# Leftover queries of two visits scored as one block in four 64x64 array tiles, ahead of the whole blocks

## The chip, the cores and the metric

One core of a Trainium2 chip. The metric is the device time of one execution in microseconds. Executions of this kernel agree within about 0.6%.

## The reference

Thresholded attention, then an MLP with a squared ReLU, all fp32:

```python
# q, k, v: (8, 8, 576, 64); tau = 0.02; w_in: (512, 2048); w_out: (2048, 512)
scores = q @ k.T / 8
scores = where(scores >= max(scores) - tau, scores, -1e9)
attn = exp(scores - max(scores)); attn = attn / (sum(attn) + 1e-9)
x = (attn @ v) -> (4608, 512)          # heads side by side
out = maximum(x @ w_in, 0) ** 2 @ w_out
```

576 queries are four whole blocks of 128 and 64 left over. That leftover is what the change is about.

## The kernel before

The work is cut into *visits*: two heads of one batch element each. A visit (from visit 8 on; the first eight are parts of visits) has five *steps*, one per block of queries: 0 to 3 are whole (128 queries of each of two heads, 64x128 array tiles), 4 is the leftover (64 queries of both heads at once, as one whole-array product with a block-diagonal `qmid`). MLP work of earlier tokens ("pieces") is spread between the steps; for all but the first *chunk* of 256 tokens, the output matrix product is made of seven smaller *products* on quarters of the matrices, of which two read `gsum`, sums that POOL makes of the squared hidden values, and two more a `gsum` that DVE makes anew. From visit 11 on the attention weights are not transposed by TensorE: DVE transposes 32x32 blocks into `turned`, and SP's queue places them in `wT` by many small transfers; four steps after a visit's last block its *mix* multiplies `wT` by v. `wT` exists once, so the next visit's placements wait for that mix to have read it.

```python
def scores(s):
    ...
    for half, u in halves:                       # two halves of 288 keys
        if i < NBLK:
            rows, lhsT = slice(u * D, (u + 1) * D), qT[u * D:(u + 1) * D, i * P:(i + 1) * P]
        else:
            rows, lhsT = slice(0, P), qmid       # leftover: whole array, half of it zeros
        nc.tensor.matmul(sc[u][:, half, 0:HALF], lhsT, kT[rows, half * HALF:(half + 1) * HALF], ...)
...
def place_blocks(vis, pair):                     # 16 transfers for blocks 0+1, 2+3, leftover each
    wb = blocks[vis, pair]
    for qb in range(4):
        for j in range(4):
            ...
            nc.sync.dma_start(out=to[:, :, at:at + 64], in_=wb[rows, j::4, :, :]...)
...
# in the loop over steps s; (m, x) is the step before
if s in mixes ...: mix(*mixes[s])                # the mix follows the scores of its step
...
turn_blocks(m, x)
if x >= 2:
    place_blocks(m, x - 2)                       # 0+1 after block 2, 2+3 after block 3, leftover last
```

## Time and profile before

| | before |
|---|---|
| time, median of 3 (later 4) | 1436.16 (1436.39) us |
| profiled span | 1426.6 us |
| TensorE (PE) busy | 1369.2 us, 96% |
| DVE, ACT, POOL busy | 62%, 31%, 63% |
| PE's wait for `wT` placed by SP, as the waits name it | 7.7 us in 5 waits |

PE is the engine to read. A line of the timeline is "start, duration, engine, source line, operation, tiles, array rows*columns, shape, count, [idle before, released by]". Durations of matmuls overlap in the pipeline and their ends are modelled, so work is priced by the distance from one start to the next.

### The profile page before, as it was taken

The page shows a single profiled execution, that of the slowest core. Times are in us where ns is not written, and L with a number is a line of the kernel's source. Part 1 is how long each engine was busy: PE and PEld are TensorE (multiplying, and loading weights), DVE is VectorE, ACT ScalarE, POOL GpSimd, SP SyncE. Part 2 cuts the span into 40 slices and gives each one's busy share as a digit, 9 for nine tenths or more (in the row PEclk, how much of TensorE's full clock was granted, in tenths as well). Part 3 has the DMA queues.
Part 4 walks back from the last instruction along what each step waited for, and adds up shares of the span by engine and source line. Part 5 has one row for each costly group of instructions (what it writes and reads, how often), then busy time and mean ns, then how long its engine had stood idle before and what let it go on. Part 6 is the DMA issues. An engine that isn't in the chain of part 4 may idle for free.

```text
span 1426.6 us, 22558 instructions
## 1 busy us (share of the span) xinstructions
PE 1369.2 (96%) x7460; PEld 1058.5 (74%) x7460; DVE 886.2 (62%) x1922; ACT 440.5 (31%) x1080; POOL 900.2 (63%) x1215
## 2 busy tenths in 40 slices
PE   5898989999999999999999999999999999999998
PEld 3676556777777777777777787777777877778887
DVE  5999986975767766757666666666666666401011
ACT  3766654222222323222232222322222232200100
POOL 2688888757676766766576757585667575422322
PEclk9999999999999999999999999999999999999999
DMA  7664431435455555554445454544444545310000
GB/s 150 131 141 115 126 101 46 83 72 98 92 104 95 110 98 107 97 110 86 93 85 106 94 108 94 107 87 98 82 101 91 109 97 104 67 30 8 8 15 16
DMA packets 397604, 127.16 MB, mean 89 GB/s; under 512 B 381488, under 2 KB 386288, under 8 KB 397488
## 3 DMA queue, kind: packets, MB, share of 16 engines
q1 hardware_dynamic: 377008, 93.02, 34.4%
q0 software_dynamic: 18096, 32.40, 8.3%
q8 instruction: 60, 0.98, 0.3%
q10 hardware_dynamic: 2384, 0.30, 0.1%
q14 instruction: 56, 0.46, 0.1%
HBM read 49.81 MB, written 9.44 MB: 42 GB/s over the span
## 4 chain that ended last, share of the span: by engine, by line
PE 78%; DVE 8%; SPq 5%; issue 3%; ACT 2%; POOL 2%; DMA 2%; POOLq 0%; DVEq 0%; ACTq 0%
PE bank L417 30%; PE bank L484 25%; PE s L212 11%; PE bank L374 10%; SPq L329 3%; SPq L337 2%; DVE st L217 2%; DVE w L240 2%; DVE turned L138 1%; DMA wT<-turned 1%; PE bank L276 1%; PE bank L451 1%; ACT w L228 1%; DVE turned L137 1%; POOL w L252 1%
## 5 line engine op out<-in xcount | busy, mean ns | idle before, releaser
L417 PE MATMUL bank<-xT,w_in_sb 128*128 128x256 f32 x2304 | 519.5, 382 | 1.6 <-ACT osb L458 1.6
L417 PEld LDWEIGHTS bank<-xT,w_in_sb 128*128 128x128 f32 x2304 | 431.9, 190 | 81.6 <-issue 21.1
L217 DVE TENSOR_REDUCE st<-s 128x1 f32<-128x576 f32 x288 | 206.6, 752 | 204.2 <-PE s L212 203.3
L240 DVE SCALAR_TENSOR_TENSOR w<-s,st,w 128x576 f32<-128x576 f32 x269 | 210.1, 814 | 121.6 <-ACT w L228 121.3
L484 PE MATMUL bank<-wo,gsum 128*128 128x256 f32 x1088 | 250.7, 384 | 4.5 <-POOL gsum L407 4.3
L252 POOL TENSOR_SCALAR w<-w,st 128x576 f32<-128x576 f32 x269 | 227.1, 851 | 26.2 <-DVE st L243 18.2
L484 PEld LDWEIGHTS bank<-wo,gsum 128*128 128x128 f32 x1088 | 205.5, 191 | 43.5 <-issue 7.1
L428 POOL TENSOR_TENSOR g<-g 128x512 f32<-128x512 f32 x144 | 152.2, 1061 | 108.3 <-ACT g L427 107.5
L225 ACT ACTIVATE st<-st 128x2 f32<-128x2 f32 (+1 forms) x160 | 32.7, 204 | 602.2 <-DVE st L217 601.6
L212 PE MATMUL s<-kT,qT 64*128 64x288 f32 x1024 | 175.7, 438 | 33.3 <-DVE w L240 16.8
L316 DVE STREAM_TRANSPOSE turned<-w 128x64 f32<-128x64 f32 (+2 forms) x400 | 173.8, 487 | 27.3 <-DMA wT<-turned 21.9
L484 PE MATMUL bank<-wo,g 128*128 128x256 f32 x816 | 187.9, 381 | 0.0
L228 ACT ACTIVATE w<-s,st 128x576 f32<-128x576 f32 x269 | 184.5, 731 | 0.6 <-issue 0.3
L374 PE MATMUL bank<-wT,vs 128*64 128x128 f32 (+7 forms) x1700 | 172.9, 356 | 10.8 <-DMA wT<-turned 7.7
L484 PEld LDWEIGHTS bank<-wo,g 128*128 128x128 f32 x816 | 153.5, 190 | 28.1 <-issue 6.4
L212 PEld LDWEIGHTS s<-kT,qT 64*128 64x128 f32 x1024 | 98.9, 190 | 93.7 <-issue 64.4
L374 PEld LDWEIGHTS bank<-wT,vs 128*64 128x64 f32 (+1 forms) x1700 | 100.6, 136 | 84.3 <-issue 37.1
L250 POOL TENSOR_SCALAR st<-st 128x2 f32<-128x2 f32 (+1 forms) x160 | 38.3, 239 | 168.6 <-DVE w L240 156.8
L427 ACT ACTIVATE g<-bank 128x512 f32<-128x512 f32 x144 | 86.1, 599 | 180.7 <-PE bank L417 180.2
L498 DVE TENSOR_TENSOR gsum<-g 128x512 f32<-128x512 f32 x34 | 22.6, 698 | 108.9 <-PE bank L484 108.9
L195 POOL COPY qmid<-qT 64x64 f32<-64x64 f32 x64 | 19.4, 303 | 84.2 <-DVE qT L191 82.3
L174 POOL DMA_DIRECT2D kl<-in_k_dram x100 | 69.6, 699 | 0.0
(70 smaller groups left out, 1109.5 us busy)
## 6 DMA issues: line engine op xcount, KB each, us to landing
wT<-turned SPq DMA_DIRECT2D x800, 72.0 KB, 2.2
out_dram<-osb POOLq DMA_DIRECT2D x34, 256.0 KB, 2.8
wo<-in_moe_w_in_dram SPq DMA_DIRECT2D x16, 512.0 KB, 4.6
wo<-in_moe_w_out_dram SPq DMA_DIRECT2D x16, 512.0 KB, 3.7
kl<-in_k_dram POOLq DMA_DIRECT2D x100, 72.0 KB, 2.6
ql<-in_q_dram POOLq DMA_DIRECT2D x100, 72.0 KB, 2.5
vs<-in_v_dram POOLq DMA_DIRECT2D x50, 128.0 KB, 3.5
wT<-turned SPq DMA_DIRECT2D x200, 20.0 KB, 1.9
```

Source lines behind the costliest of these rows:

```text
L174: nc.gpsimd.dma_start(out=to, in_=src)
L212: nc.tensor.matmul(sc[u][:, half, 0:HALF], lhsT, kT[rows, half * HALF:(half + 1) * HALF], start=True, stop=True)
L217: nc.vector.tensor_reduce(out=mx[:, u:u + 1], in_=sc[u][:, :, 0:HALF], axis=AX.XY, op=ALU.max)
L228: nc.scalar.activation(out=w[:, u, :].rearrange("p (h k) -> p h k", h=2), in_=sc[u][:, :, 0:HALF], func=AF.Exp, bias=bias[:, u:u + 1], sca ...
L240: nc.vector.scalar_tensor_tensor(out=wu, in0=sc[u][:, :, 0:HALF], scalar=thr[:, u:u + 1], in1=wu, op0=ALU.is_ge, op1=ALU.mult, accum_out=s ...
L252: nc.gpsimd.tensor_scalar(out=w[:, u, :], in0=w[:, u, :], scalar1=z[:, u:u + 1], scalar2=rcp[:, u:u + 1], op0=ALU.add, op1=ALU.mult)
L316: nc.vector.transpose(wb[:, at:at + k1 - k0, i % 2, :], w[:, u, k0 * 32:k1 * 32].rearrange("p (k q) -> p k q", q=32))
L374: nc.tensor.matmul(ps[u * D:(u + 1) * D, :], vs[n % 2][rows, u * (NBLK + 1) + c, :], wT[rows, NBLK if c == NBLK else u * (NBLK + 1) + c, a ...
L417: nc.tensor.matmul(h[:, x % 2, :], w_in_sb[:, c, f * P:(f + 1) * P], xT[:, c, at:at + TCH], start=(c == 0), stop=(c == NMC - 1))
L427: nc.scalar.activation(out=to, in_=h, func=AF.Relu)
L428: nc.gpsimd.tensor_tensor(out=to, in0=to, in1=to, op=ALU.mult)
L484: nc.tensor.matmul(to, left[:, f, :], wo[:, slot, f, :], start=(f == 0), stop=(f == HF - 1))
```

## The change

The visits 12 to 35 are taken in pairs. The leftovers of a pair (four heads, 64 queries each) become one step of two PSUM tiles, in four 64x64 array tiles: head u takes the rows, visit v the columns. It comes first of the pair's nine steps (ten before). For that q's leftover rows get loads of their own (`q_left`, 8 small ones a pair), k's transpose exists twice, `wT` gets 64 more columns so that the odd visit's leftover has its own place, loads and placements get an explicit schedule, and the ring of MLP inputs shrinks from six chunks to five to pay for the memory. Its core:

```diff
-    wT = const.tile([P, NC9, S], FP32, name="wT")
+    ODD, ONE, LEFT, TWO = 0, REST, REST + 2 * P, 2 * REST + 2 * P
+    wT = const.tile([P, NC9, S + REST], FP32, name="wT")
-    kT = const.tile([P, S], FP32, name="kT")
-    RING = 6 * TCH
+    kT = [const.tile([P, S], FP32, name=f"kT{i}") for i in range(2)]
+    RING = 5 * TCH
...
+        if i == NBLK and paired(vis):
+            for half in range(2):
+                for v_ in range(2):
+                    for u in range(2):
+                        rows, cols = slice(u * D, (u + 1) * D), slice(v_ * D, (v_ + 1) * D)
+                        term(u, half, rows, qmid[rows, cols], kT[v_], cols)
...
+    def paired(n):
+        return n >= 3 * HP
+    for n in range(len(visits)):
+        if paired(n):
+            visits[n] = visits[n][0], ([] if n % 2 else [NBLK]) + list(range(NBLK))
...
+            place_at[s + (2 if paired(n - 1) else 3)].append((n, 2, (0, 1)))
+            place_at[s + 3] += [(n, 2, (2, 3)), (n, 0)]
+            place_at[s + 5].append((n, 1))
+            place_at[s + 8].append((n + 1, 0))
+            place_at[s + 9].append((n + 1, 1))
...            (further: the schedule of loads and transposes, the layout in mix)
```

More of the change, by code (lines that the diff above doesn't have):

```diff
@@ L84 @@
     assert at + 2 * S <= 3 * HF * HD
+    q_left = const.tile([P, 2, REST // 32, 32], FP32, name="q_left")
     qT = const.tile([P, S], FP32, name="qT")
-    kT = const.tile([P, S], FP32, name="kT")
-    RING = 6 * TCH
+    kT = [const.tile([P, S], FP32, name=f"kT{i}") for i in range(2)]
+    RING = 5 * TCH
     xT = const.tile([P, NMC, RING], FP32, name="xT")
@@ L151, with rows_32 @@
     loads = deque()
+    def rows_32(t, n, m):
+        b, h = divmod(visits[n][0], HP)
+        return t[b, 2 * h + m // 2, :, (m % 2) * 32:(m % 2) * 32 + 32].rearrange("(c p) d -> p c d", p=32)
     def load_qk(n):
-        b, h = divmod(visits[n][0], HP)
-        h *= 2
+        if by_dma(n):
+            load_part(k, n)
+            load_part(q, n)
+            return
         for x, t in ((rows_of(n)[1], k), (rows_of(n)[0], q)):
             for m in range(4):
-                src = t[b, h + m // 2, :, (m % 2) * 32:(m % 2) * 32 + 32].rearrange("(c p) d -> p c d", p=32)
-                to = x[m * 32:(m + 1) * 32, :, :]
-                if by_dma(n):
-                    loads.append((to, src))
-                    continue
+                src, to = rows_32(t, n, m), x[m * 32:(m + 1) * 32, :, :]
                 queue = nc.scalar if n == 0 and m % 2 else nc.sync
@@ L169, in load_qk, with load_part, load_left, some_loads @@
                     queue.dma_start(out=to[:, 0:last, :], in_=src[:, S // 32 - last:, :])
-    def some_loads(count):
-        for _ in range(min(count, len(loads))):
+    def load_part(t, n):
+        x = rows_of(n)[0 if t is q else 1]
+        loads.extend((x[m * 32:(m + 1) * 32, :, :], rows_32(t, n, m)) for m in range(4))
+    def load_left(n):
+        for m in range(4):
+            for v_ in range(2):
+                loads.append((q_left[m * 32:(m + 1) * 32, v_, :, :], rows_32(q, n + v_, m)[:, NBLK * P // 32:, :]))
+    def some_loads():
+        for _ in range(min(1 + (len(loads) > 8), len(loads))):
             to, src = loads.popleft()
             nc.gpsimd.dma_start(out=to, in_=src)
+    def arrived(t):
+        assert all(x[0].tensor.name != t.tensor.name for x in loads)
     def load_v(n):
@@ L179, in load_v @@
         t = vs[n % 2]
-        queue = nc.gpsimd if by_dma(n) else nc.sync
+        todo = []
         for u in range(2):
             at = u * (NBLK + 1)
-            queue.dma_start(out=t[:, at:at + NBLK, :],
-                              in_=v[b, h + u, 0:NBLK * P, :].rearrange("(c p) d -> p c d", p=P))
+            todo.append((t[:, at:at + NBLK, :], v[b, h + u, 0:NBLK * P, :].rearrange("(c p) d -> p c d", p=P)))
             for half in range(2):
-                queue.dma_start(out=t[half * D:(half + 1) * D, at + NBLK, :], in_=v[b, h + u, NBLK * P:S, :])
+                todo.append((t[half * D:(half + 1) * D, at + NBLK, :], v[b, h + u, NBLK * P:S, :]))
+        if paired(n):
+            loads.extend(todo)
+            return
+        for to, src in todo:
+            (nc.gpsimd if by_dma(n) else nc.sync).dma_start(out=to, in_=src)
     def prep(n):
-        for to, rows in zip((qT, kT), rows_of(n)):
-            nc.vector.transpose(to, rows.rearrange("p c d -> p (c d)"))
+        prep_part(q, n)
+        prep_part(k, n)
         if NBLK in visits[n][1]:
@@ L195, in prep, with prep_part, prep_left @@
                 nc.gpsimd.tensor_copy(out=qmid[rows, u * D:(u + 1) * D], in_=qT[rows, NBLK * P:S])
+    def prep_part(t, n):
+        to, rows = (qT, rows_of(n)[0]) if t is q else (kT[n % 2], rows_of(n)[1])
+        arrived(rows)
+        nc.vector.transpose(to, rows.rearrange("p c d -> p (c d)"))
+    def prep_left():
+        arrived(q_left)
+        nc.vector.transpose(qmid, q_left.rearrange("p v c d -> p (v c d)"))
     weights = {}
@@ L201, in scores, with term @@
         vis, i = steps[s]
-        n = 2 if i < NBLK else 1
+        n = 2 if i < NBLK or paired(vis) else 1
         sc = [psum.tile([P, 2, 512], FP32, tag=f"s{u}", name=f"s{u}") for u in range(n)]
-        halves = [(half, u) for half in range(2) for u in range(n)]
-        if early():
-            halves.sort(key=lambda x: x[1])
-        for half, u in halves:
-            if i < NBLK:
-                rows, lhsT = slice(u * D, (u + 1) * D), qT[u * D:(u + 1) * D, i * P:(i + 1) * P]
-            else:
-                rows, lhsT = slice(0, P), qmid
-            nc.tensor.matmul(sc[u][:, half, 0:HALF], lhsT, kT[rows, half * HALF:(half + 1) * HALF],
-                             start=True, stop=True)
+        def term(u, half, rows, lhsT, keys, to=slice(0, P)):
+            nc.tensor.matmul(sc[u][to, half, 0:HALF], lhsT, keys[rows, half * HALF:(half + 1) * HALF],
+                             start=True, stop=True)
+        if i == NBLK and paired(vis):
+            for half in range(2):
+                for v_ in range(2):
+                    for u in range(2):
+                        rows, cols = slice(u * D, (u + 1) * D), slice(v_ * D, (v_ + 1) * D)
+                        term(u, half, rows, qmid[rows, cols], kT[v_], cols)
+        elif i == NBLK:
+            for half in range(2):
+                term(0, half, slice(0, P), qmid, kT[vis % 2])
+        else:
+            halves = [(half, u) for half in range(2) for u in range(n)]
+            if early():
+                halves.sort(key=lambda x: x[1])
+            for half, u in halves:
+                rows = slice(u * D, (u + 1) * D)
+                term(u, half, rows, qT[rows, i * P:(i + 1) * P], kT[vis % 2])
         st = pool.tile([P, 7, 2], FP32, tag="st", name="st", bufs=4)
@@ L291 @@
     blocks = {}
-    N1 = 2 * P + REST
     def turn_blocks(vis, i):
@@ L301, in turn_blocks @@
         two = i < NBLK
+        both = two or paired(vis)
         M = KB - 2
@@ L304, in turn_blocks @@
             at = len(blocks) % 2 * NB
-            size = 2 * KB * 2 if two else KB + 2
+            size = 2 * KB * (1 + two) if both else KB + 2
             blocks[vis, i // 2] = turned[:, at:at + size * 32].rearrange("p (k u q) -> p k u q", u=1 + two, q=32)
         wb = blocks[vis, i // 2]
-        if two:
-            odd = M if i >= 2 else KB
+        if both:
+            odd = M if i in (2, 3) else KB
             parts = [(0, 0, M, 0), (0, M, KB, 2 * M + 2 - odd), (1, M, KB, odd), (1, 0, M, KB + 2)]
-            if i < 2:
+            if odd == KB:
                 parts[0:2] = [(0, 0, KB, 0)]
@@ L317, in turn_blocks, with place_blocks @@
                                 w[:, u, k0 * 32:k1 * 32].rearrange("p (k q) -> p k q", q=32))
-    def place_blocks(vis, pair):
+    def place_blocks(vis, pair, which=range(4)):
         wb = blocks[vis, pair]
-        for qb in range(4):
+        for qb in which:
             rows = slice(qb * 32, qb * 32 + 32)
@@ L327, in place_blocks @@
                 if pair < NBLK // 2:
-                    at = pair * N1 + qb * 64
+                    at = (ONE, TWO)[pair] + qb * 64
                     nc.sync.dma_start(out=to[:, :, at:at + 64], in_=wb[rows, j::4, :, :].rearrange("p c u q -> p c (u q)"))
+                    continue
+                at = LEFT + qb % 2 * 32
+                if paired(vis):
+                    at = at if qb < 2 else ODD + qb % 2 * 32
+                    nc.sync.dma_start(out=to[:, :, at:at + 32], in_=wb[rows, j::4, 0, :])
                 else:
@@ L334, in place_blocks @@
                     n = len(range(first, KB if qb < 2 else 2 * KB, 4))
-                    c, at = first // 4, 2 * P + qb % 2 * 32
+                    c = first // 4
                     first += 2 if qb < 2 else -KB
@@ L378, in mix @@
         above, below = slice(0, D), slice(D, P)
+        arrived(vs[n % 2])
         if not by_dma(n):
@@ L387, in mix @@
             return
+        n1, n2 = 2 * P + REST, 2 * P
+        at = ODD if paired(n) and n % 2 else ONE
         one, two = (next_bank() for x in range(2))
+        groups = (one[:, 0:n1], at, (above, below)), (two[:, 0:n2], TWO, (below, above))
         for c in range(NBLK):
-            for ps, at in ((one[:, 0:N1], 0), (two[:, 0:S - N1], N1)):
+            for ps, x, _ in groups:
                 for u in range(2):
-                    term(ps, u, c, at, first=(c == 0))
-        for ps, at, places in ((one[:, 0:N1], 0, (above, below)), (two[:, 0:S - N1], N1, (below, above))):
+                    term(ps, u, c, x, first=(c == 0))
+        for ps, x, places in groups:
             for u, rows in enumerate(places):
-                term(ps, u, NBLK, at, rows, last=True)
-        put(n, 0, one[:, 0:2 * P], True)
-        put(n, NBLK * P, one[:, 2 * P:N1], False)
-        put(n, 2 * P, two[:, 0:S - N1], True)
+                term(ps, u, NBLK, x, rows, last=True)
+        put(n, 0, one[:, ONE - at:ONE - at + 2 * P], True)
+        left = ODD if at == ODD else LEFT - at
+        put(n, NBLK * P, one[:, left:left + REST], False)
+        put(n, 2 * P, two[:, 0:n2], True)
     def square_half(lo):
@@ L520 @@
     visits += [(g_, list(range(NBLK + 1))) for g_ in range(HP, NPAIR)]
+    def paired(n):
+        return n >= 3 * HP
+    for n in range(len(visits)):
+        if paired(n):
+            visits[n] = visits[n][0], ([] if n % 2 else [NBLK]) + list(range(NBLK))
     steps = [(n, i) for n in range(len(visits)) for i in visits[n][1]]
@@ L536 @@
         if by_dma(n):
-            mixed = {NBLK: (0, 4)}
+            mixed = {visits[n][1][-1]: (0, 4)}
         else:
@@ L541 @@
             first, lag = mixed[i]
-            cols = slice(first * P, min((i + 1) * P, S))
+            cols = slice(first * P, S if by_dma(n) else min((i + 1) * P, S))
             mixes[s + lag] = (n, cols)
@@ L628, in end_rounding @@
             load_weights(p + RAW)
+    place_at, load_at, prep_at = ({s: [] for s in range(END + 10)} for x in range(3))
+    for s, (n, i) in enumerate(steps):
+        if not by_dma(n) or i != visits[n][1][0] or paired(n) and n % 2:
+            continue
+        nxt = n + (2 if paired(n) else 1)
+        more = nxt < len(visits)
+        if paired(n):
+            place_at[s + (2 if paired(n - 1) else 3)].append((n, 2, (0, 1)))
[3 more added lines that the diff above has]
+            place_at[s + 9].append((n + 1, 1))
+            prep_at[s].append(lambda n=n: prep_part(q, n))
+            load_at[s].append(lambda n=n: load_part(q, n + 1))
+            load_at[s + 2].append(lambda n=n: load_v(n))
+            prep_at[s + 4].append(lambda n=n: prep_part(q, n + 1))
+            load_at[s + 4].append(lambda n=n: load_v(n + 1))
+        else:
+            place_at[s + 3].append((n, 0))
+            place_at[s + 4].append((n, 1))
+            place_at[s + 5].append((n, 2))
+        if more:
+            a, b, c, d = (s + 1, s + 5, s + 7, s + 8) if paired(n) else (s + 1, s + 2, s + 4, s + 4)
+            load_at[a].append(lambda n=nxt: load_part(k, n))
+            if paired(n):
+                load_at[a].append(lambda n=nxt: load_left(n))
+            prep_at[b].append(lambda n=nxt: prep_part(k, n))
+            load_at[b].append(lambda n=nxt: load_part(k, n + 1))
+            if not paired(n):
+                load_at[b].append(lambda n=nxt: load_left(n))
+            load_at[b].append(lambda n=nxt: load_part(q, n))
+            prep_at[c].append(prep_left)
+            prep_at[d].append(lambda n=nxt: prep_part(k, n + 1))
     load_qk(0)
@@ L653 @@
                 load_qk(n + 2)
-            elif not short and at == 1 and more:
+            elif not short and at == 1 and not by_dma(n):
                 load_qk(n + 1)
@@ L685 @@
             threshold(n, i)
-            if last and more and not lay:
-                assert not loads
-                prep(n + 1)
+            for fn in prep_at[s] + load_at[s]:
+                fn()
             if lay and now:
@@ L698 @@
             turn_blocks(m, x)
-            if x >= 2:
-                place_blocks(m, x - 2)
-        some_loads(1)
+        for what in place_at[s]:
+            place_blocks(*what)
+        some_loads()
         fill(quarter)
-        some_loads(1)
+        some_loads()
         if on and at_once:
@@ L706 @@
         fill(quarter)
-        some_loads(1)
+        some_loads()
         fill(quarter)
-        some_loads(1)
+        some_loads()
         if on:
@@ L718 @@
                 load_v(n)
-            elif last and more and n >= 2 * HP:
+            elif last and n >= 2 * HP and not by_dma(n):
                 load_v(n + 1)
```

## The prediction

> **What bounds the kernel now.** I read the page's busy table and its 40 slices first:
>
> ```profile
> PE 1369.2 (96%) x7460; PEld 1058.5 (74%) x7460; DVE 886.2 (62%) x1922; ACT 440.5 (31%) x1080; POOL 900.2 (63%) x1215
> ...
> PE   5898989999999999999999999999999999999998
> ```
>
> TensorE is full nearly everywhere; its gaps lie in the first seven slices (about 250 us), the attention of the first batch, whose instructions the change leaves alone. The paired visits (visit 12 on, of 0 to 35) begin after roughly 300 us, and the last block of attention ends near 1230 us. So the stretch that matters is 330 to 1230 us. Its busy times, then all of PE's own waits in it:
>
> ```profile
> core 0: us, PE busy (x) PEld busy (x) DVE busy (x) ACT busy (x) POOL busy (x), PEclk, DMA share, GB/s
> 330.00:1230.00 900.00, 892.62 (x4671) 689.89 (x4671) 590.71 (x1346) 251.25 (x630) 604.36 (x867) 1.00 0.49 96
> ```
>
> ```profile
> PE bank L374 <- DMA wT<-turned: 4.9, 4, 1.5
> PE bank L484 <- POOL gsum L407: 2.2, 3, 1.2
> ```
>
> PE is idle for 900 - 892.6 = 7.4 us of 900; the waits name 4.9 + 2.2 of them. DVE (66%), POOL (67%) and ACT (28%) have room and the clock is full. Hence a shorter time can come from (a) fewer PE cycles, worth their full size, and (b) those few waits, at most some 7 us, plus one of 2.8 us at the last mix (1261 us, also `wT` by DMA). Work saved on DVE, ACT or POOL is worth nothing by itself.
>
> A busy PE is a modelled busy, so I price PE work by start-to-start distances in the timeline of a quiet place:
>
> ```profile
> 702.99 1.13 PE L212 MATMUL s<-kT,qmid 128*128 128x288 f32 x4
> 703.96 7.07 PE L417 MATMUL bank<-xT,w_in_sb 128*128 128x256 f32 x32
> 710.96 1.24 PE L212 MATMUL s<-kT,qT 64*128 64x288 f32 x8
> 712.13 7.17 PE L417 MATMUL bank<-xT,w_in_sb 128*128 128x256 f32 x32
> 719.24 1.24 PE L212 MATMUL s<-kT,qT 64*128 64x288 f32 x8
> ```
>
> and in the tail, where no block of another shape interrupts the MLP:
>
> ```profile
> 1369.71 27.79 PE L417 MATMUL bank<-xT,w_in_sb 128*128 128x256 f32 x128
> 1397.33 3.62 PE L484 MATMUL bank<-wo,g 128*128 128x256 f32 x16
> ```
>
> Each fp32 matmul of the source is two instructions. Readings:
> - MLP alone: (1397.33 - 1369.71)/128 = 0.216 us for 256 columns, 0.84 ns a column; 32 of them 6.91 us.
> - A leftover block (four instructions, whole array): 703.96 - 702.99 = 0.97 us = 4 x 0.2425, exactly its columns. It costs nothing extra.
> - A whole block (eight instructions in 64x128 tiles, two abreast): 712.13 - 710.96 = 1.17 us, where four rounds of 288 columns are 0.97. So 0.20 extra inside.
> - The MLP run after a leftover block and before a whole block takes 710.96 - 703.96 = 7.00 us; the run between two whole blocks 719.24 - 712.13 = 7.11. Against 6.91, each border with a tiled block costs a further 0.10. A tiled block among MLP work thus costs about 0.97 + 0.20 + 2 x 0.10 = 1.37 us.
>
> **The skill.** "TensorEngine Tiling (Array Packing)", Tiling Modes, Key Properties: changing the tiling mode drains TensorE. The trace agrees: about 0.4 us per tiled block, none for the untiled leftover block. The same section says that different tiles work in parallel, and "TensorE: Matmul & The Clock Gate", Part 3 (Packing small matmuls) that row and column packing compose. Here the trace has four 64x64 tiles already, the last terms of every mix:
>
> ```profile
> 741.50 0.76 PE L374 MATMUL bank<-wT,vs 64*64 64x320 f32 x8
> 742.18 0.48 PE L484 MATMUL bank<-wo,gsum 128*128 128x256 f32 x1
> ```
>
> Eight instructions, four of 320 and four of 256 columns, in 0.68 us. By the 0.84 ns a column they would take 1.94 us one by one, 0.97 two abreast, 0.54 four abreast. 0.68 is four abreast with 0.14 for the change of mode, although two column tiles stream different data out of the same rows, as the new block's do. Third, "Perfetto Trace Analysis", Identifying the Most-Contended Engine, warns that matmul busy is a bad measure of headroom and LDWEIGHTS busy a better one: PEld is at 77% here, so "full" means "always occupied", not "at its peak"; this is why I use start-to-start distances.
>
> **The change, part by part.**
> 1. *PE scores.* 24 visits, so 12 pairs. Removed: 24 leftover blocks, 24 x 0.97 = 23.3 us. Added: 12 blocks of 16 instructions in four 64x64 tiles: four rounds of four, 4 x 0.2425 = 0.97, plus the same change of mode as a whole block has (the built instruction order puts MLP work on both sides of all twelve), 0.40: 12 x 1.37 = 16.4 us. Net **-6.8 us**. The order confirms that nothing else on PE changes: 1152 + 952 MLP matmuls, 512 of whole blocks and all mix terms stay; the neighbourhoods of whole blocks and mixes stay too. So half the array work saved (11.6 us) is eaten in part by twelve drains (4.8 us).
> 2. *DVE, ACT, POOL per block.* The passes over 128x576 stay equal in number. Gone are one set of small ones per pair: 12 x (205 + 281 ns) on ACT, 12 x (154 + 164) on DVE, 12 x 263 on POOL, and 48 `qmid` copies on POOL. Added: 12 transposes of 128x128 on DVE. All in slack: 0.
> 3. *POOL's DMA issues.* The 8 loads per pair for `q_left` are new:
>
> ```profile
> L186 POOL DMA_DIRECT2D vs<-in_v_dram x100 | 54.5, 561 | 0.0
> L195 POOL COPY qmid<-qT 64x64 f32<-64x64 f32 x64 | 19.4, 303 | 84.2 <-DVE qT L191 82.3
> ```
>
> 96 x about 0.56 us (the small loads' row) = 54 us, less 48 x 0.30 = 14.5 and 3 us: POOL +36 us over the stretch, 67% to about 72%. POOL makes `gsum`, which a product waits for two or four pieces after a chunk's last input piece. I allow **+2 us** of new PE waits on it (2.2 now).
> 4. *Placing the blocks.* SP issues of `wT<-turned` fall from 96 to 80 a pair, and the leftovers' are out of the way early. The queue now:
>
> ```profile
> L329 SPq DMA_DIRECT2D wT<-turned x709: 585/612/1832, 346.7 to 1230.0; - x178
> ...
> SPq L329 <- PE bank L374: 150.0, 23, 7.2
> ```
>
> One issue takes 0.61 us, so a visit's 48 take 29 us plus 2.2 to land. They can start only after the previous mix has read `wT` (that is the 150 us), and the next mix comes five steps later, about 39 us (900 us / 23 visits). That margin of 8 us is lost in four visits (4.9 us) and at the end (2.8 us). After: in an even visit 24 issues follow the previous odd mix (15 us) and 16 two steps later; in an odd visit 16 and 16. Steps also grow from 7.8 to about 8.6 us, since 108 steps carry the work of 120. I expect most of the 7.7 us to go: **-5 us**.
> 5. *The ring.* Five chunks for six: the copy into it waits for a mix that PE runs after the last read of the old chunk anyway, so no new wait. `kT` twice: k can be transposed while the other visit still reads; no PE wait on `kT` was left in this stretch. 0.
>
> Sum: -6.8 + 2 - 5 = -9.8 us, from 1436.2: **1426 us**.
>
> **Rivals.**
> - *The four tiles do not run abreast.* Two abreast would make eight rounds, 1.94 + 0.4, and 12 x 0.97 = 11.6 us more: about 1438. Against it: the 0.68 us above.
> - *POOL delays the squares or gsum.* Its loads wait in order behind transposes of the same step, and it has more issues. If each of the 14 or so chunks in the stretch lost 1 us on gsum: about 1438. For it: the wait is in the profile already. Against: 28% of POOL stays free.
> - *The chain of a step becomes the bound.* A score needs its two PSUM tiles free of the threshold before it. In this stretch PE waited for that not once, and steps get longer. I give it little; if 1 us in half of 108 steps, about 1480.
> - *All waits vanish and drains cost less* (0.2 a block): about 1418.
>
> **Range and chances.** The three timed runs span 1430.9 to 1439.2, so the base alone is uncertain by some 4 us; the terms by about 6. I say 1417 to 1437 in 8 of 10. A gain over 2% (28.7 us) needs more than the whole 23.3 us of leftover blocks, so it would have to come from somewhere I have not seen: 0.03. A loss over 2%: 0.02. Within: 0.95.
>
> **What would show it.** The twelve new blocks: 16 instructions from 1.1 to 1.25 us start to start, MLP runs beside them 0.1 longer at that border. PE busy down by 6 to 10 us in the whole page, span down by about 10. PE's wait on `wT` in the stretch below 2 us and none at the last mix; its wait on gsum below 6. SP issues of `wT` down by 192. The prediction is wrong if the new block takes over 2 us, if `L240` scores begin to wait on DVE, or if PE's idle time in the stretch passes 15 us.

## The result

The changed kernel takes 1416.76 us (median of 4, 1411.82 to 1416.86) against 1436.39 us. The ratio is 0.9859, 95% interval 0.9823 to 0.9896. Ratios here are the mean time of one kernel's runs over that of the other's of the same rounds, so not quite the ratio of the medians. That is 20 us less, where 10 were predicted; the time lies just below the range. The gain, 1.4%, is clear of noise, but under the 2% from which a verdict here says faster.

The page after, the same two rows as before, and the busy times of the same stretch (attention now ends near 1212 us):

```profile
PE 1358.1 (96%) x7556; PEld 1039.6 (74%) x7556; DVE 882.3 (63%) x1898; ACT 436.1 (31%) x1052; POOL 933.1 (66%) x1251
...
PE   5898989999999999999999999999999999999998
```

```profile
330.00:1212.00 882.00, 879.36 (x4727) 671.60 (x4725) 590.51 (x1326) 247.40 (x603) 631.37 (x893) 1.00 0.51 100
```

PE stays the bound; its idle time in the stretch falls from 7.4 us of 900 to 2.6 us of 882. POOL is at 71.6%. The four largest of PE's ten waits after, over the whole run (engine, line, what released it: us in total, times, longest):

```profile
PE s L240 <- DVE w L285: 16.2, 11, 3.6
PE s L240 <- DVE kT L224: 8.5, 1, 8.5
PE s L240 <- DVE wo L285: 7.2, 5, 3.0
PE bank L538 <- POOL gsum L461: 6.1, 4, 3.5
```

The row for `wT` (7.7 us before) is gone; gsum's went from 4.3 to 6.1. Most of that rise is one wait at 286 us, ahead of the stretch (2.1 us before, 3.5 after); inside the stretch gsum's row goes from 2.2 to 2.6. The first new block, at 276 us, waits 1.8 us for `qmid` from DVE; all waits of scores on DVE together are 33.8 us before and 33.7 after. SP issued 1008 transfers into `wT` for 1200 before, 192 fewer. A new block in the timeline after:

```profile
655.56 3.72 PE L538 MATMUL bank<-wo,gsum 128*128 128x256 f32 x16
659.21 1.20 PE L240 MATMUL s<-kT,qmid 64*64 64x288 f32 x16
660.34 1.99 PE L538 MATMUL bank<-wo,gsum 128*128 128x256 f32 x8
```

660.34 - 659.21 = 1.13 us for sixteen instructions: four abreast. Last, the end of attention, before and after:

```profile
1257.76 0.75 PE L374 MATMUL bank<-wT,vs 128*64 128x320 f32 x2
1261.32 4.75 PE L374 MATMUL bank<-wT,vs 128*64 128x320 f32 x38 [2.82 <-DMA wT<-turned]
1266.00 2.21 PE L417 MATMUL bank<-xT,w_in_sb 128*128 128x256 f32 x9
```

```profile
1243.98 4.79 PE L423 MATMUL bank<-wT,vs 128*64 128x320 f32 x40
1248.69 3.50 PE L471 MATMUL bank<-xT,w_in_sb 128*128 128x256 f32 x15
```

The last mix takes 1266.00 - 1257.76 = 8.24 us before and 1248.69 - 1243.98 = 4.71 after. The difference is 3.5 us, though the profile calls only 2.82 of it idle. That is the first sight of what the prediction missed.

**Where the time went.** I gave each PE matmul the time from its start to the next matmul's start and summed by kind over both traces. These sums leave nothing out (the time after the last matmul's start stands in the last row):

| us, start to start | before | after | change |
|---|---|---|---|
| leftover blocks | 31.1 | 21.9 | -9.2 |
| 128x64 part of the mixes placed by DMA (25) | 113.2 | 100.8 | -12.4 |
| MLP input matmuls | 511.3 | 513.0 | +1.7 |
| products and output | 461.0 | 463.9 | +2.9 |
| whole blocks | 172.5 | 171.3 | -1.2 |
| other mix terms, transposes, both ends of the run | 137.5 | 138.8 | +1.3 |
| span | 1426.6 | 1409.8 | -16.8 |

An undisturbed mix has 4.03 us in its 128x64 part, 25 of them 100.8 us. Before, seven were longer (5.94, 6.29, 6.20, 5.44, 4.89, 4.26 and, at the end, 7.56 us, and an eighth by 0.07); after, none by more than 0.06.

### The profile page after: what moved, and what is told of

Same layout as the page of the kernel before. It is cut to its first block, busy times and chain, and to the rows that moved or that the text cites. A ratio compares the mean times of both kernels' runs of the same rounds, so it can differ in the third digit from the quotient of the medians.

```text
span 1409.8 us, 22708 instructions
## 1 busy us (share of the span) xinstructions
PE 1358.1 (96%) x7556; PEld 1039.6 (74%) x7556; DVE 882.3 (63%) x1898; ACT 436.1 (31%) x1052; POOL 933.1 (66%) x1251
## 4 chain that ended last, share of the span: by engine, by line
PE 85%; DVE 6%; POOL 3%; ACT 2%; issue 2%; DMA 1%; SPq 1%; POOLq 0%; ACTq 0%; DVEq 0%
PE bank L471 33%; PE bank L538 28%; PE s L240 12%; PE bank L423 10%; DVE turned L142 1%; DVE st L262 1%; PE bank L321 1%; DVE w L285 1%; PE bank L505 1%; DVE turned L141 1%; ACT w L273 1%; POOL w L297 1%; ACT wT L322 1%; POOL gsum L461 0%; POOL g L482 0%
## 5 line engine op out<-in xcount | busy, mean ns | idle before, releaser
L240 PE MATMUL s<-kT,qT 64*128 64x288 f32 x1024 | 175.9, 440 | 31.5 <-DVE w L285 15.6
L361 DVE STREAM_TRANSPOSE turned<-w 128x512 f32<-128x512 f32 (+2 forms) x388 | 168.8, 490 | 12.9 <-DMA wT<-turned 11.6
L295 POOL TENSOR_SCALAR st<-st 128x2 f32<-128x2 f32 (+1 forms) x148 | 34.9, 236 | 206.4 <-DVE w L285 196.0
L423 PE MATMUL bank<-wT,vs 128*64 128x128 f32 (+7 forms) x1700 | 168.4, 356 | 3.0 <-ACT wT L322 2.4
L240 PEld LDWEIGHTS s<-kT,qT 64*128 64x128 f32 x1024 | 98.9, 191 | 92.0 <-issue 61.5
L423 PEld LDWEIGHTS bank<-wT,vs 128*64 128x64 f32 (+1 forms) x1700 | 95.7, 136 | 76.8 <-issue 25.9
L191 POOL DMA_DIRECT2D vs<-in_v_dram x144 | 90.8, 635 | 0.0
```

The costliest lines, as they stand in the source:

```text
L191: nc.gpsimd.dma_start(out=to, in_=src)
L240: nc.tensor.matmul(sc[u][to, half, 0:HALF], lhsT, keys[rows, half * HALF:(half + 1) * HALF], start=True, stop=True)
L361: nc.vector.transpose(wb[:, at:at + k1 - k0, i % 2, :], w[:, u, k0 * 32:k1 * 32].rearrange("p (k q) -> p k q", q=32))
L423: nc.tensor.matmul(ps[u * D:(u + 1) * D, :], vs[n % 2][rows, u * (NBLK + 1) + c, :], wT[rows, NBLK if c == NBLK else u * (NBLK + 1) + c, a ...
```

## The experiments

Eleven runs were made, two of them of the two kernels again. Ratios below are against the kernel before on the same chip in the same rounds.

**Both kernels again** (`r_before`, `r_after`; no edit). Expected of the first:

> The kernel before, unchanged, again: a second trace of it and a null for the timing. Theory W (the trace of before lost 12.4 us of TensorE time in its mixes: 25 runs of 32 mix instructions sum to 113.2 us start to start, 25 x 4.03 would be 100.8; my prediction took the 7.7 us that the view of waits names as the whole of it and gave 5 back) expects that loss again, 8 to 16 us of mixes above 100.8 us. Rival N (the stalls were an accident of one execution): under 4 us here. Time ratio to before 1.000 within 0.003 for both.

Expected of the second:

> The changed kernel, unchanged, again. Theory W: mixes at 100.8 us with no stall at all, four-tile blocks at 14.1 us together, ratio of times 0.985 to 0.990 (the traces differ by 16.8 of 1426.6 us, 0.988). Rival N: some stalled mixes also here. If the ratio stays at 0.986 while the traces differ by 0.988, some 3 us of the gain lie outside what the two traces show.

Measured: 0.9995 (0.9969 to 1.002) and 0.9864 (0.9841 to 0.9887). The mixes of `r_before` are 116.3 us, 15.5 above the undisturbed 100.8, at the same places (about 350, 428, 507, 585 and the last); those of `r_after` 100.8, the twelve blocks 14.1. The stalls are no accident. The second trace of before shows one thing more, at its last mix; the second fence is the stretch 1266 to 1282 us of it (PEclk is the third figure from the right), the third the same 16 us of the first trace of before:

```profile
1267.58 0.75 PE L374 MATMUL bank<-wT,vs 128*64 128x320 f32 x2
1271.06 6.44 PE L374 MATMUL bank<-wT,vs 128*64 128x320 f32 x38 [2.73 <-DMA wT<-turned]
1277.42 4.80 PE L417 MATMUL bank<-xT,w_in_sb 128*128 128x256 f32 x21
```

```profile
1266.00:1282.00 16.00, 13.27 (x69) 9.11 (x68) 0.42 (x1) 1.36 (x4) 0.69 (x2) 0.89 0.15 42
```

```profile
1256.00:1272.00 16.00, 13.18 (x77) 9.53 (x76) 0.42 (x1) 1.36 (x4) 1.62 (x3) 1.00 0.15 42
```

After a wait of the same length the granted clock was 0.89 over 16 us instead of 1.00, and the 38 instructions took 6.44 instead of 4.75 us. So a stall can cost again after it has ended, in some executions: start to start, the 38 took 1.7 us more here.

**Fewer placements, nothing else** (`e_half_left`), the kernel before with half of the leftover placements left out. Its output is wrong, which doesn't matter for the time.

```diff
-        for qb in range(4):
+        for qb in range(4 if pair < NBLK // 2 else 2):
```

> The kernel before with 8 of the 16 leftover placements of each visit left out (the result is wrong on purpose: half of the leftover queries get old weights); TensorE, DVE, ACT and POOL do exactly what they did. SP issues 40 a visit for 48, 4.9 us less just ahead of the mix. Theory W (a stalled mix costs its full lost time, so the stalls of before were worth 12 to 15 us): mixes at 101 us, time down by 11 to 16 us, ratio 0.989 to 0.993. Rival S (as in my prediction: worth about 5 us): ratio 0.996 to 0.997. Rival H (TensorE's idle time merely moves elsewhere, as in the order alone): mixes at 101 us but ratio above 0.997.

Measured: 1421.58 us, ratio 0.990 (0.9883 to 0.9916): 14.4 us less with the same PE instructions. Mixes 100.8 us. Its PE waits from the third row on:

```profile
PE s L212 <- DVE wo L240: 7.0, 5, 3.0
PE bank L484 <- POOL gsum L407: 4.3, 4, 2.1
PE bank L374 <- ACT wT L277: 2.4, 10, 0.2
```

No `wT` by DMA is left, gsum is at 4.3 as before. Theory W stands and both rivals fall: the stalls were worth 14 us, not 5, and nothing took their place. This is the experiment that decides.

**The order alone** (`e_order_alone`), leftover first in its own visit, unpaired, untiled, with the double place in `wT` and an early load of the leftover q. Core of the edit:

```diff
+            visits[n] = visits[n][0], [NBLK] + list(range(NBLK))
...
+            elif x == 1:
...
+                place_blocks(m, 0)
+            elif x == 3:
+                place_blocks(m, 1)
+            if moved(m) and x == 0 and not late:
+                place_blocks(m, 2)
```

> The leftover block comes first in its own visit, with its own early load of q and a second place in wT for odd visits; no pairing, the leftover scores stay two whole-array matmuls per visit, ring of 5 chunks. PE has the work of before exactly. Theory W (the waits for wT by DMA in the mix are worth their full lost time, and it is the early placement that removes them): mixes near 101 us, time down by 10 to 14 us, ratio 0.990 to 0.993. Rival S (as in the prediction: only about 5 us to be had from these waits): ratio 0.996. Rival P (the waits go because pairing cuts the SP issues from 96 to 80 a pair, not because of the order; here they stay 96): mixes still above 108 us, ratio 0.998 or more.

Measured: 1437.64 us, ratio 1.0007, and a wrong result (relative error 0.094), my mistake: visit 12's leftover q was written over visit 11's before use. Mixes 101.9, so the stalls went but for one of 1.2 us, but 14.4 us of new waits (start to start, beyond the streaming) stood ahead of the leftover blocks: moved to the head of the visit, they need q and k that were transposed only just before. Mended:

```diff
+    kT = [const.tile([P, S], FP32, name=f"kT{i}") for i in range(2)]
...
+            if moved(n) and at == 0:
+                prep_part(q, n)
+            if moved(n + 1) and by_dma(n) and at == (3 if moved(n) else 4) and more:
+                prep_left()
+                prep_part(k, n + 1)
```

> The order alone once more, mended: kT twice, k and the leftover q transposed one step before the visit ends and q after its leftover block (as the change does it), and the leftover q of visit 12 no longer written over visit 11's (that made the first try wrong in one visit). PE has the matmuls of before exactly, 24 whole-array leftover blocks, SP 96 issues a pair. Theory W (the late landing of wT is a matter of order, and each stalled mix is worth its full lost time): mixes at 101 us, no waits of 14 us before the leftover blocks as in the first try, time down by 10 to 14 us, ratio 0.990 to 0.993. Rival (the order only moves the wait to other places): ratio 0.997 to 1.001 again.

Measured: 1428.93 us, correct, ratio 0.9951 (0.9932 to 0.997), 7 us less. Mixes 101.5, one stall left in the first moved visit. Half of the gain is missing, and the trace has waits that the kernel before does not have (8.9 us together: the two rows here, 0.8 more on g, 1.4 on `p1s` and 0.2 on `p5s`; gsum's wait fell from 4.3 to 3.1):

```profile
PE s L232 <- DVE qT L209: 3.9, 2, 2.1
...
PE bank L439 <- ACT g L449: 2.6, 2, 1.6
```

So neither theory got its number. The order does remove the stalls, with 96 issues a pair as before, so Rival P falls; in this version it does not keep the gain. Fewer issues alone (`e_half_left`) remove them as well; which of the two does it in the changed kernel is not shown. The changed kernel is 0.9864, some 12 us below this one, of which the pairing's PE work explains about 7 (below). That the rest is the waits just shown is likely, not shown.

**More issues in the changed kernel** (`e_more_issues`):

```diff
-            place_at[s + 5].append((n, 1))
+            place_at[s + 5] += [(n, 1), (n, 1)]
-            place_at[s + 9].append((n + 1, 1))
+            place_at[s + 9] += [(n + 1, 1), (n + 1, 1)]
```

> The changed kernel with the second half of every visit's wT (16 transfers) placed twice, the same data again: SP issues 112 a pair for 80. Theory W: SP's queue is what makes wT late; 16 more issues at 0.61 us are 9.8 us more, which uses up the margin of about 9 us (even visits) and 9 (odd), so stalls of 0 to 4 us return in about half of the 24 mixes: mixes at 110 to 130 us for 100.8, time up by 10 to 30 us, ratio 0.993 to 1.006. Rival (the stalls of before had another cause): mixes at 101 us, ratio 0.986.

Measured: 1571 us, ratio 1.0934. The direction was right, the size wrong by five times: every one of the 24 mixes after the first lost 1.5 to 11 us, and the mixes together took 257.3 us. Rows of PE's and SP's waits (the view books three more of the 24 to DVE, 21.1 us):

```profile
PE bank L423 <- DMA wT<-turned: 86.5, 21, 8.5
```

```profile
SPq L373 <- PE bank L423: 92.4, 12, 9.0
```

I had counted one late arrival per mix. But SP may place again only after the late mix has read, so lateness is handed on; and 21 of the 24 stalls were followed by a stretch of halved clock (mean clock of the run 0.950 against 0.993); the three without one were the shortest, with 1.5, 1.7 and 3.0 us lost. How much each of the two adds I did not separate. What the run shows is that SP's queue is the cause and how near to its limit it is. Slower transfers are not: the median from issue to landing of these placements was 2.4 us, against 2.3 in the changed kernel.

**The block's work twice** (`e_twice`):

```diff
-            for half in range(2):
+            for half in (0, 1, 0, 1):
```

> The changed kernel with the matmuls of the four-tile blocks issued twice over, the second time over the first. PE is the bound in that stretch, so each added round counts in full: 12 x 4 rounds x 0.2425 = 11.6 us, ratio 0.9945 (0.9864 + 11.6/1436). Rival (a part of PE's work lies in the shadow of other waits): less than 6 us. Rival (the tiles do not run four abreast): 23 us or more, ratio over 1.002.

Measured: 1426.01 us, ratio 0.9931 (0.991 to 0.9951), so 9.6 us over the changed kernel's 0.9864; in the trace the twelve blocks go from 14.13 to 25.77 us, by 11.6. One of them:

```profile
666.08 2.17 PE L240 MATMUL s<-kT,qmid 64*64 64x288 f32 x32
668.18 1.99 PE L538 MATMUL bank<-wo,gsum 128*128 128x256 f32 x8
```

2.10 us for 32 instructions against 1.13 for 16: 0.97 us of streaming and 0.16 of change inside a block. Four abreast, and PE cycles count (nearly) in full.

**The block's loops turned** (`e_by_visit`):

```diff
-            for half in range(2):
-                for v_ in range(2):
+            for v_ in range(2):
+                for half in range(2):
```

> The changed kernel with the loops of the four-tile block turned: all of one visit first, then all of the other, so that at most two of the four tiles can run at once; same instructions, same result. Theory of four abreast: each of the 12 blocks takes 4 more rounds of 0.2425 us = 0.97 us longer, about 2.1 us instead of 1.17, time up by 11.6 us against the changed kernel (ratio 0.994 against before if that is 0.986). Rival (the four never ran abreast, or the hardware looks ahead over the order): block unchanged at 1.17 us, time as the changed kernel.

Measured: 1417.6 us, ratio 0.9864, the same as the changed kernel, and the block still takes 1.15 us. My expectation of it was wrong, not for want of four tiles abreast but because the hardware did not keep my order. The start of one block, in a window that ends 0.19 us after its first start:

```profile
664.75 0.38 PE L538 MATMUL bank<-wo,gsum 128*128 128x256 f32 x1
665.06 0.49 PE L240 MATMUL s<-kT,qmid 64*64 64x288 f32 x4
```

Four matmuls run there. In the built order the first eight instructions are all of the first visit, on two tiles alone; the trace has the second visit's first two start 0.02 us after the first visit's first two, ahead of six earlier instructions (the third to start is the one that carries a wait on DVE's semaphore, which in the built program is the second visit's first). So this run cannot price two tiles abreast.

**The ring alone** (`e_ring5`), the kernel before with `RING = 5 * TCH`:

> The kernel before with the ring of MLP inputs cut from six chunks to five and nothing else. The prediction put this at 0, since the copy into the ring waits for a mix that PE runs after the last read of the old chunk anyway: ratio 1.000 within 0.003, ACT's waits unchanged. Rival (copies wait for the ring and delay the MLP): ratio over 1.003.

Measured: 1437.32 us, ratio 1.0009 (0.9994 to 1.0024). No effect, as predicted. Its trace is a third look at the stalls: 14.8 us above 100.8. (The other way, six chunks in the changed kernel, did not fit: the pool would need 210.3 KB per partition and 207.9 are there.)

**Fewer loads of v** (`e_fewer_loads`):

```diff
-            for half in range(2):
-                todo.append((t[half * D:(half + 1) * D, at + NBLK, :], v[b, h + u, NBLK * P:S, :]))
+        for half in range(2):
+            todo.append((t[half * D:(half + 1) * D, NBLK::NBLK + 1, :], v[b, h:h + 2, NBLK * P:S, :].rearrange("u p d -> p u d")))
```

> The changed kernel with four loads of v a visit for six (the two heads' halves of the last rows in one transfer): 48 DMA issues of about 0.6 us less on POOL in the paired visits, some 29 us of POOL. Theory G (the waits of products on gsum, 6.1 us now and 4.3 before, come from POOL being late because of its extra issues): the wait falls to 3 to 5 us, time down by 1 to 3 us, ratio 0.984 to 0.986. Rival (gsum is late for the order of the squares and products, whatever POOL issues): wait 6 us as before, ratio 0.9864.

Measured: 1416.64 us, ratio 0.9865. POOL's busy time fell from 933.1 to 904.9 us and the wait on gsum from 6.1 to 4.4, but no time came of it that the rounds could tell. All of the fall is the one wait near 290 us (3.5 to 1.6 us); in the stretch the row is 2.6 and 2.8. So POOL's issues delay gsum at that one place, and no effect is shown elsewhere.

**Product 2 ahead of 5 and 6** (`e_two_first`), on top of the fewer loads, a try at a faster version:

```diff
-    PRODUCTS = ("1", "5", "6", "2", "7", "4", "3")
+    PRODUCTS = ("1", "2", "5", "6", "7", "4", "3")
```

> The changed kernel with the fewer loads of v and with product 2, which needs no gsum, put ahead of products 5 and 6, which do: 1.7 us more for POOL. Theory G2 (gsum is late by the order of products): the waits on gsum (6.1 us, 4.4 with fewer loads) go nearly to 0, time down by 3 to 5 us, ratio 0.983 to 0.984. Rival: product 7 now follows its own new gsum too closely and waits on DVE instead; ratio 0.986 or above.

Measured: 1422.12 us, ratio 0.9905 (0.989 to 0.992), slower by 6 us than the changed kernel. The rival is right, and the row shows it:

```profile
PE bank L538 <- DVE gsum L552: 9.5, 5, 3.3
```

Product 7 waits for the gsum that DVE makes anew after product 5, and product 2 no longer stands between. No version beat the changed kernel.

## Why the prediction was wrong

- *What bounds the kernel* was right: PE before, PE after, and DVE, ACT and POOL work without worth.
- *PE scores, -6.8 us*: right. The block takes 14.1/12 = 1.175 us where 1.17 was taken over from a whole block; the leftover row falls by 9.2. The MLP rows rise by 1.7 + 2.9 = 4.6. Of that, 3.1 are longer waits on gsum (1.2 of them only moved here: one such wait stood in the row of whole blocks before), the waits of scores on DVE fall by about 0.6 in these rows, and about 2 are left for the new borders (12 x 0.20 = 2.4 was the estimate). So about -9.2 + 2 = -7.
- *POOL's issues, +2 us*: right in sum, in part by luck. POOL came to 71.6%, and over the whole run the wait on gsum rose by 1.8. But the prediction counted from the 2.2 of the stretch, and there it rose only to 2.6; the rest is the one wait at 286 us.
- *The ring and the second kT, 0*: right for the ring by its own run.
- *Placing the blocks, -5 us*: this step failed. The mechanism (SP's queue has too little time between two mixes, the change gives it fewer issues and an earlier start) is shown by `e_half_left` and `e_more_issues`. The term was mis-sized: 12.4, 15.5 and 14.8 us in three traces with the old placement, 14.4 us in time. Two errors made it 5, and a third hid them. First, I took the named idle time, 7.7 us, for what the stalls cost. In the trace of before, five stalls are named. In each, two instructions of one half of a tile pair had gone ahead without their partners and bought nothing for their 0.54 us (5 x 0.54 = 2.7), and the modelled ends of the last one hide about 0.17 us each (0.9). Three shorter stalls (0.86, 0.23 and 0.07 us, 1.2 together) have no idle time at all, because the modelled end of the matmul before covers them. 7.7 + 2.7 + 0.9 + 1.2 = 12.5, the 12.4 but for rounding. In two of the three traces a halved clock after the last stall adds some 1.7 us. Second, I gave back a third of the 7.7 for caution although my own margins said that the stalls should all go; they did. Third, the margin of 8 us before the change was not there. It set 29 + 2.2 us of placing against 39 us from mix to mix. In the trace of before SP's first placement goes out 4.8 us or more after the mix before it has started, since that mix must have read `wT`; and from there to the last landing 33.3 to 35.1 us pass, not 31, since the issues stand about 0.64 us apart and the queue pauses once or twice on the way. That makes 38 us or more, where from mix to mix are mostly 40.5 us, 37.1 to 37.3 for four of the stalled ones and 35.2 for the last. One of the four, out of the chain that ended last (start, us, what):

```profile
495.51 0.60 SPq L337
496.15 1.85 DMA wT<-turned
498.01 0.14 issue
498.14 4.75 PE bank L374 x29
```

This mix began at 495.94, its last placement landed at 498.01, 2.07 us later, and it lost 2.17 us. In all eight longer mixes of this trace the lost time is that lateness (from -0.03 to 3.43 us) plus 0.10 or 0.11 us, so the late landings account for the whole 12.4.

The signs that the prediction named came out as follows: the new block, PE's idle time and the 192 issues as said, no wait on `wT`, PE busy down by 11.1 us (6 to 10 said) and the span by 16.8 (10 said). That `L240` scores wait on DVE could not serve as a sign, since scores did so before the change too, outside the stretch; in the stretch none does.

Put together from the runs: about -14.4 (stalls, in time) - 7 + 2 = -19.4 us, against -19.5 by `r_after` (0.9864 of 1436); the nearness is luck, as each term is good to a us or two. The first pair of traces shows only -16.8: that trace of before is of an execution of 1428.45 us, faster than all four timed ones (1430.88 at best), and its stalls were the least of the three. Differences of a few us between traces also come from short stretches of halved clock in the first 300 us, in both kernels; I did not pursue them.

The range failed with this term: it ended at 1417, where all named waits vanish and the drains cost little. It left no room for a wait that costs more than its name.

## What to carry to other kernels

Price a stall as you price work: the distance between two starts with the stall, less the same distance without it, over all instances, including those with no named wait. When two tiles run abreast, a wait that stops one of them can waste the other's time as well (here 38 instructions after a stall took 4.68 us where all 40 take 4.71). In the margin of a queue that waits for its reader, count the reader's own time, here 4.8 us. And before crediting a tiling with a gain, look at what the new order does to the queues: here fewer and earlier transfers were worth twice the net PE work saved (14.4 us and about 7).

## What the Trainium skill lacked or had wrong

- "TensorE: Matmul & The Clock Gate", Part 3 (Packing small matmuls), The mechanism, has matmuls in "strict FIFO, no reordering". In `e_by_visit` the matmuls of two free tiles started 0.02 us after the first ones, ahead of six instructions built before them that wanted busy tiles; the block took 1.15 us where strict order would give about 2.1 (an estimate: eight rounds of 0.2425 us and the change of mode).
- "TensorEngine Tiling (Array Packing)", Key Properties, names the drain at a change of mode and gives it no price. Here a tiled block among untiled work took 0.16 to 0.20 us beyond its columns inside, and 0.10 more at each border.
- "DMA: Bandwidth & Descriptors", Issuing engines are not separate DMA queues, calls the sequencer's time to start a transfer usually small beside the transfer. Here an issue took 0.61 of the 2.2 us from its start to the landing, and issues add up on one queue: 48 a visit, 29 us, made `wT` late, and 8 fewer a visit were worth 14.4 us (`e_half_left`).
- No page that I read says that the idle time named before a matmul understates a stall where tiles run abreast: 7.7 us named, 12.4 lost in the trace of before.
